# Reordered first loads, a first weight cast in four parts, a first v cast on two engines, and re-timed fillers

## The chip, the cores and the metric

The kernel runs on one core of a Trainium2 chip. The metric is device time in microseconds (us), the median of several executions. "The trace" is the record of one profiled execution, in which times count from the start of the span. The span (about 297 us here) is a little shorter than the timed execution. Engines are abbreviated as in the profile: PE is TensorE, PEld its weight loads, DVE VectorE, ACT ScalarE, POOL GpSimd, SP SyncE, which issues the transfers.

## The reference

The computation is a retention layer (attention with a decay in place of softmax) followed by a feed-forward layer with a squared ReLU. Cut to what matters:

```python
# q, k, v: [8 batches, 8 heads, 576, 64] float32; w_in [512, 2048]; w_out [2048, 512]
scores = q @ k.T / 8
ret    = (scores * Dmat) @ v                  # Dmat: gamma_h ** (i - j), lower triangle
x      = ret, heads side by side              # [4608, 512]
h      = x @ w_in
out    = maximum(h, 0)**2 @ w_out             # [4608, 512]
```

## The kernel before

The tokens are handled in 18 groups of 256. Each group's q, k, v are loaded, cast to float16, transposed, turned into scores, masked, and multiplied out to `xT`. Then 64 matmuls on `w_in` (called feed-forward matmuls below), the squared ReLU, and the output matmuls on `w_out` follow. In the first groups the output matmuls are 128x512. Later ones replace part of them by sums of matrices (a Strassen scheme), so that VectorE forms sums `gS` for TensorE.

The order of all instructions is fixed when the program is built. A list scheduler simulates the five engines with a **modelled duration** for each task and always starts the ready task of smallest key. A duration in the model is not a wait on the chip, but it decides the order in which instructions are put into each engine's queue.

```python
FIRST = ["p0", "p2", "w0", "w1", "w2", ..., "w7", "p4", "p6"]     # loads, in this order
...
for i in range(WARM):        # 40 filler matmuls, taken only when nothing else is ready
    fill.append(add("PE", 10 ** 6, 0.43 if i < 8 else 0.216, warm, ...))
...
# a pair of groups: k, q, v, one load each of 512 KB
loaded[name, u] = loaded[name, u + 1] = dma_task(0, 1.6 if loaded else 3.0, fn, ...)
...
# a weight block of 1 MB: cast in two halves, one by GpSimd, one by ScalarE
for j, eng in enumerate(("POOL", "ACT")): ...
...
# the casts of a pair: both halves of the first pair's v on VectorE
eng = "DVE" if (lead if name != "v" else (lead or e)) else "POOL"
```

Loads called w0 to w3 are the blocks of `w_in`, w4 to w7 those of `w_out`. The "third pair" is the one loaded after the weights.

## Time and profile before

| what | before |
|---|---|
| median of 3 runs | 299.49 us (299.16 to 299.77) |
| span of the profiled run | 296.8 us |
| TensorE busy | 285.9 us, 96% |
| VectorE, ScalarE, GpSimd busy | 196.5, 187.3, 92.1 us |
| DMA engines full | from 3 to about 46 us |

The busy shares say that TensorE is the resource, and that only some 11 us of the span are not covered by it. Where those lie is read in the slices and stretches that the prediction shows. In a timeline line, the columns are the start, the time that the piece took, engine, source line, operation, output and inputs, and the count. A bracket gives the engine's idle time before the piece, and what ended it.

### The profile page before, as it was taken

Reading aid. Unit: us, or ns where it says so; the run is one execution under the profiler, and the core shown is the slowest. Engines: PE = TensorE matmul, PEld = TensorE weight load, DVE = VectorE, ACT = ScalarE, POOL = GpSimd, SP = SyncE. Lnnn points to the kernel's source line nnn. Section 1 sums busy time; section 2 is a strip of 40 time slices with the busy share of each in tenths; the row PEclk is TensorE's granted clock in tenths of the full one; section 3 lists DMA queues with packets and bytes.
Section 4 is the critical chain, followed back from the end, with each engine's and each line's share of the span. In section 5 each row is a group of like instructions: output and inputs, shape, how many; then the busy total and the mean of one; then the engine's idle time right before and its main releaser. Section 6 shows DMA issues by size and latency. Waiting matters only on the chain.

```text
span 296.8 us, 10046 instructions
## 1 busy us (share of the span) xinstructions
PE 285.9 (96%) x4320; PEld 233.8 (79%) x4320; DVE 196.5 (66%) x414; ACT 187.3 (63%) x353; POOL 92.1 (31%) x127
## 2 busy tenths in 40 slices
PE   8969989999999999999999999999999999999995
PEld 3558745687878888888888888888888888888874
DVE  4597479859395939593949598766777876462410
ACT  4348753484857666657576666666676856658861
POOL 4433396434242424152514142233433410000000
PEclk9999999999999999999999999999999999999999
DMA  7999997999887989898979597989999960101012
GB/s 202 310 388 385 362 300 207 185 224 164 209 162 195 185 195 207 198 179 202 176 181 177 142 181 188 184 187 202 184 217 203 180 140 2 73 3 71 2 71 73
DMA packets 139261, 54.14 MB, mean 182 GB/s; under 512 B 118096, under 2 KB 130640, under 8 KB 139216
## 3 DMA queue, kind: packets, MB, share of 16 engines
q1 hardware_dynamic: 138768, 52.97, 81.6%
q8 instruction: 34, 0.56, 0.8%
q10 hardware_dynamic: 448, 0.52, 0.6%
q14 instruction: 11, 0.09, 0.1%
HBM read 36.70 MB, written 9.44 MB: 155 GB/s over the span
## 4 chain that ended last, share of the span: by engine, by line
PE 67%; DMA 12%; DVE 10%; ACT 6%; issue 2%; POOL 2%; SPq 0%; DVEq 0%; POOLq 0%
PE ph L807 29%; PE po L900 26%; DVE gS L878 6%; PE po L848 5%; PE psO L331 4%; DMA wo<-in_moe_w_out_dram 4%; ACT gT L825 3%; DMA pair<-in_k_dram 3%; ACT rl L815 3%; DMA wi<-in_moe_w_in_dram 3%; DMA pair<-in_v_dram 2%; DVE rT L629 1%; PE psc L331 1%; PE psS L331 1%; POOL qx L391 1%
## 5 line engine op out<-in xcount | busy, mean ns | idle before, releaser
L807 PE MATMUL ph<-xT,w_in 128*128 128x256 f16 x1152 | 139.0, 273 | 1.1 <-POOL w_in L313 1.1
L807 PEld LDWEIGHTS <-w_in 128*128 128x128 f16 x1152 | 111.2, 98 | 15.7 <-POOL w_in L313 1.4
L815 ACT ACTIVATE rl<-ph 128x512 f16<-128x512 f32 x144 | 83.9, 588 | 49.2 <-PE ph L807 45.7
L825 ACT ACTIVATE gT<-rl 128x512 f16<-128x512 f16 x112 | 70.5, 630 | 3.5
L878 DVE TENSOR_TENSOR gS<-gT 128x512 f16<-128x512 f16 x60 | 28.9, 485 | 42.6 <-ACT gT L825 42.0
L900 PEld LDWEIGHTS <-gS 128*128 128x128 f16 x480 | 45.7, 98 | 8.5 <-DVE gS L878 3.0
L900 PE MATMUL po<-wT,gS 128*128 128x256 f16 x360 | 49.2, 273 | 1.1 <-DVE gS L878 1.1
L355 POOL TENSOR_TENSOR v<-v,vdec_full 128x512 f16<-128x512 f32 x24 | 25.6, 1067 | 46.8 <-DMA v<-in_v_dram 43.0
L900 PEld LDWEIGHTS <-gT 128*128 128x128 f16 x360 | 34.9, 98 | 4.3
L343 POOL CAST kq<-k 128x512 f16<-128x512 f32 x28 | 19.1, 684 | 44.7 <-DMA k<-in_k_dram 39.0
L900 PE MATMUL po<-w_out,gT 128*128 128x256 f16 x240 | 31.1, 273 | 0.0
L343 POOL CAST kq<-q 128x512 f16<-128x512 f32 x28 | 18.7, 667 | 26.7 <-DMA q<-in_q_dram 26.6
L827 DVE TENSOR_TENSOR gT<-rl 128x512 f16<-128x512 f16 x32 | 16.2, 510 | 13.8 <-ACT rl L815 13.4
L848 PE MATMUL po<-w_out,gT 128*128 128x512 f16 (+1 forms) x112 | 22.9, 349 | 0.2 <-POOL w_out L313 0.2
L690 DVE TENSOR_TENSOR xT<-psO,gam_full 128x512 f16<-128x512 f32 x28 | 18.4, 684 | 4.6 <-PE psO L331 4.5
L913 ACT COPY u<-po 128x256 f32<-128x256 f32 x30 | 11.0, 366 | 13.4 <-PE po L900 13.3
L878 DVE TENSOR_TENSOR gS<-gS,gT 128x512 f16<-128x512 f16 x30 | 18.1, 604 | 1.0
L629 DVE TENSOR_TENSOR rT<-psc,mask 128x512 f16<-128x512 f32 x28 | 18.6, 680 | 0.3 <-PE psc L331 0.3
L923 DVE TENSOR_TENSOR o<-po,u 128x256 f32<-128x256 f32 x30 | 12.5, 418 | 9.3 <-PE po L900 5.3
L878 DVE TENSOR_TENSOR gS<-gT,gS 128x512 f16<-128x512 f16 x30 | 16.4, 548 | 1.0
L848 PEld LDWEIGHTS <-gT 128*128 128x128 f16 x112 | 10.6, 98 | 7.9 <-issue 0.4
L900 PE MATMUL po<-w_out,gS 128*128 128x256 f16 x120 | 15.8, 273 | 0.0
(78 smaller groups left out, 264.2 us busy)
## 6 DMA issues: line engine op xcount, KB each, us to landing
out_dram<-o SPq DMA_DIRECT2D x31, 256.0 KB, 2.7
k<-in_k_dram SPq DMA_DIRECT2D x24, 256.0 KB, 4.6
q<-in_q_dram SPq DMA_DIRECT2D x24, 256.0 KB, 4.4
v<-in_v_dram SPq DMA_DIRECT2D x24, 256.0 KB, 4.5
wi<-in_moe_w_in_dram SPq DMA_DIRECT2D x4, 1024.0 KB, 9.4
wo<-in_moe_w_out_dram SPq DMA_DIRECT2D x4, 1024.0 KB, 9.6
pair<-in_k_dram SPq DMA_DIRECT2D x4, 512.0 KB, 8.0
pair<-in_q_dram SPq DMA_DIRECT2D x4, 512.0 KB, 7.4
```

The costliest lines, as they stand in the source:

```text
L331: nc.tensor.matmul(out_, lhsT=lhsT, rhs=rhs, start=start, stop=True, skip_group_check=True, tile_position=(64 * row, 64 * col))
L343: op(out=out_.rearrange("p (n b a d) -> p n b a d", n=2, b=2, a=2), in_=in_.rearrange("p (n a b) d -> p n b a d", n=2, a=2))
L355: nc.gpsimd.tensor_tensor(out=t, in0=tile_of["v32", u], in1=vdec[kind].rearrange("p (h o) -> p h o", o=1).to_broadcast([P, H, D]), op=ALU. ...
L629: nc.vector.tensor_tensor(out=r, in0=tile_of["psc", g][:, :, cols(s)].rearrange("p a (n i) -> p a n i", i=64), in1=mask.rearrange("p (o r ...
L690: nc.vector.tensor_tensor(out=tile_of["x", g][:, :, s * P:(s + 1) * P].rearrange("p n (c i) -> p c n i", c=2), in0=tile_of["psO", g][:, :, ...
L807: nc.tensor.matmul(tile_of["ph", g, fb][:, j, :], lhsT=w_in16[:, m, fi * P:(fi + 1) * P], rhs=tile_of["x", g][:, m, :], start=(m == 0), st ...
L815: nc.scalar.activation(out=t, in_=tile_of["ph", g, fb], func=ACTF.Relu)
L825: nc.scalar.activation(out=t, in_=rl, func=ACTF.Square)
L827: nc.vector.tensor_tensor(out=t, in0=rl, in1=rl, op=ALU.mult)
L848: nc.tensor.matmul(tile_of["po", u, lo], lhsT=tile_of["g", g][:, fi, s * P:(s + 1) * P], rhs=w_out16[:, fi, lo:hi], start=(fi == 0), stop= ...
L878: nc.vector.tensor_tensor(out=Sx(k, h), in0=in0(h), in1=in1(h), op=op)
L900: nc.tensor.matmul(tile_of["pb", g, bank], lhsT=left(i), rhs=right[:, i, :], start=(start and i == 0), stop=(i == HF - 1), skip_group_chec ...
```

## The change

The intent is to start feed-forward work earlier. TensorE stood idle for 2.28 us between 16 and 22 us, so the first weight block is taken ahead of the second pair's v and cast in four quarters. The first pair's v is shared by two engines, the transposes no longer wait for v's cast, and fillers stand where their cold (slow) duration puts them. Beside that, one line alters the modelled duration of a load.

```diff
-    FIRST = ["p0", "p2", "w0", "w1", ..., "w7", "p4", "p6"]
+    FIRST = ["k0", "q0", "v0", "k2", "q2", "w0", "v2", "w1", ..., "w7", "k4", "q4", "v4", "k6", "q6", "v6"]
...
-        fill.append(add("PE", 10 ** 6, 0.43 if i < 8 else 0.216, warm, ...
+        fill.append(add("PE", 10 ** 6, 1.75 if i == 0 else 0.43 if i < 15 else 0.216, warm, ...
...
-            loaded[name, u] = loaded[name, u + 1] = dma_task(0, 1.6 if loaded else 3.0, fn, ...
+        loaded[name, u] = loaded[name, u + 1] = dma_task(0, 1.81 if loaded else 2.9, fn, ...
...
+        parts = 2 if i == 0 else 1                     # weight block 0 in four casts
+        for part in range(parts): ...
...
-                eng = "DVE" if (lead if name != "v" else (lead or e)) else "POOL"
+                eng = "DVE" if (e if name == "v" else lead) else "POOL"
...
-                xs[name].append(add(eng, base + i + e / 2, dur, fc, ...
+                xs[name].append(add(eng, base + (7 if name == "v" else i + e / 2), dur, fc, ...
...
+        return w[:2] if fi < 2 else w                  # the first matmuls need two quarters only
```

More of the change, by code (lines that the diff above doesn't have):

```diff
@@ L227 @@
     PAIRED = 8
-    FIRST = ["p0", "p2", "w0", "w1", "w2", "w3", "w4", "w5", "w6", "w7", "p4", "p6"]
+    FIRST = ["k0", "q0", "v0", "k2", "q2", "w0", "v2", "w1", "w2", "w3", "w4", "w5", "w6", "w7", "k4", "q4", "v4", "k6", "q6", "v6"]
     sched = Schedule(dict(ff=4, prS=1, prO=1, g=3, ld=5, wst=4, kq=7, v16=7, rT=4, x=3, rl=3, o=4, p1=1, u2=1, u4=1,
@@ L243 @@
     for i in range(WARM):
-        fill.append(add("PE", 10 ** 6, 0.43 if i < 8 else 0.216, warm, deps=fill[-1:], acq=() if fill else ("ff",)))
+        fill.append(add("PE", 10 ** 6, 1.75 if i == 0 else 0.43 if i < 15 else 0.216, warm, deps=fill[-1:], acq=() if fill else ("ff",)))
     sched.free("ff", fill[-1:])
@@ L282, in add_load, with add_load_pair, fn @@
             loaded[name, u] = dma_task(0, 1.2 if loaded else 2.1, fn, acq=("ld",) if n == 0 else ())
-    def add_load_pair(u):
+    def add_load_pair(name, u):
         b, c = units[u][1:]
-        for n, (name, src) in enumerate((("k", k), ("q", q), ("v", v))):
-            def fn(n=n, name=name, src=src):
-                if name != "q":
-                    tile_of["stage", u] = stage.tile([P, 2, H, 2 * D], FP32, name="pair", tag="wst")
-                x = tile_of[name + "32", u] = tile_of["stage", u][:, n % 2]
-                nc.sync.dma_start(out=x, in_=src[b, :, c * P:(c + 2) * P, :].rearrange("h (p e) d -> p h (e d)", e=2))
-            loaded[name, u] = loaded[name, u + 1] = dma_task(0, 1.6 if loaded else 3.0, fn,
-                                                             acq=("wst",) if name != "q" else ())
+        n = "kqv".index(name)
+        def fn():
+            if name != "q":
+                tile_of["stage", u] = stage.tile([P, 2, H, 2 * D], FP32, name="pair", tag="wst")
+            x = tile_of[name + "32", u] = tile_of["stage", u][:, n % 2]
+            nc.sync.dma_start(out=x, in_=(k, q, v)[n][b, :, c * P:(c + 2) * P, :].rearrange("h (p e) d -> p h (e d)", e=2))
+        loaded[name, u] = loaded[name, u + 1] = dma_task(0, 1.81 if loaded else 2.9, fn, acq=("wst",) if name != "q" else ())
     def add_weight(i):
@@ L309, in add_weight, with fc @@
         halves = []
-        for j, eng in enumerate(("POOL", "ACT")):
-            def fc(j=j, eng=eng):
-                s = tile_of["w", i]
-                (nc.gpsimd.tensor_copy if eng == "POOL" else nc.scalar.copy)(
-                    out=dst[:, 2 * j:2 * j + 2], in_=s[:, 2 * j:2 * j + 2])
-            halves.append(add(eng, -50 + i, 1.2 if eng == "POOL" else 1.0, fc, deps=[t]))
+        parts = 2 if i == 0 else 1
+        for part in range(parts):
+            sl = slice(part * 512 // parts, (part + 1) * 512 // parts)
+            for j, eng in enumerate(("POOL", "ACT")):
+                def fc(j=j, eng=eng, sl=sl):
+                    s = tile_of["w", i]
+                    (nc.gpsimd.tensor_copy if eng == "POOL" else nc.scalar.copy)(
+                        out=dst[:, 2 * j:2 * j + 2, sl], in_=s[:, 2 * j:2 * j + 2, sl])
+                halves.append(add(eng, -50 + i, (1.05 if eng == "POOL" else 1.0) / parts, fc, deps=[t]))
         sched.free("wst", halves)
@@ L319 @@
     for x in FIRST:
-        (add_load_pair if x[0] == "p" else add_weight)(int(x[1:]))
+        if x[0] == "w":
+            add_weight(int(x[1:]))
+        else:
+            add_load_pair(x[0], int(x[1:]))
     for u in range(NU):
@@ L378, in add_unit_pair @@
             for e in range(2):
-                eng = "DVE" if (lead if name != "v" else (lead or e)) else "POOL"
+                eng = "DVE" if (e if name == "v" else lead) else "POOL"
                 def fc(name=name, e=e, eng=eng):
-                    if e == 0:
+                    if (name + "x", u) not in tile_of:
                         tile_of[name + "x", u] = cast.tile([P, 2, H * D], FP16, name=name + "x", tag="kq16")
@@ L393, in add_unit_pair @@
                 dur = (dict(POOL=1.1, DVE=0.6) if name == "v" else dict(POOL=0.62, DVE=0.4))[eng]
-                xs[name].append(add(eng, base + i + e / 2, dur, fc, deps=[loaded[name, u]] + xs[name],
+                xs[name].append(add(eng, base + (7 if name == "v" else i + e / 2), dur, fc, deps=[loaded[name, u]],
                                     acq=() if e else ("kq",)))
+            if xs[name][0]["eng"] == xs[name][1]["eng"]:
+                sched.need(xs[name][1], xs[name][0])
         sched.free("wst", xs["k"] + xs["q"])
@@ L404, in ft @@
                         nc.tensor.transpose(t[:, e, x, :], tile_of[name + "x", u][:, e, x * P:(x + 1) * P], ident)
-            t = add("PE", base + 2 + i, 0.45, ft, deps=[xs[name][-1]], acq=("ff",))
+            t = add("PE", base + 2 + i, 0.45, ft, deps=xs[name], acq=("ff",))
             if name == "q":
@@ L421, in add_unit_pair @@
             sched.free("ff", es)
-        T["kvx", u] = [xs["k"][-1], xs["v"][-1]]
+        T["kvx", u] = xs["k"] + xs["v"]
     def add_ret_pair(g):
@@ L791, with wcast_of @@
     T["ff2"] = []
+    def wcast_of(fi):
+        w = wcast[fi // 4]
+        return w[:2] if fi < 2 else w
     def add_ff(g):
@@ L809, in add_ff @@
                 f1.append(add("PE", base + (nf * fb + j) * n, 0.01 + 0.2133 * n, f,
-                              deps=[T["x", u] for u in us] + wcast[(nf * fb + j) // 4] + f1[-1:],
+                              deps=[T["x", u] for u in us] + wcast_of(nf * fb + j) + f1[-1:],
                               acq=("ff",) if j == 0 else ()))
```

## The prediction

> **What bounds the kernel now.** I began with the busy slices of the page, to find the phases.
>
> ```profile
> PE   8969989999999999999999999999999999999995
> DMA  7999997999887989898979597989999960101012
> ```
>
> TensorE is at nine tenths almost everywhere; the soft slices are the third (14.8 to 22.3 us) and the sixth. The DMA engines are full through the sixth slice (44.5 us). So I asked for busy time per stretch over the first 50 us, and added the idle of TensorE after that: 0.37 us in 60 to 70, 0.8 in 80 to 100, 0.6 in 100 to 150, 0.5 in 150 to 200, next to none to 290. What a start-up change can win lies before 45 us.
>
> ```profile
> core 0: us, PE busy (x) PEld busy (x) DVE busy (x) ACT busy (x) POOL busy (x), PEclk, DMA share, GB/s
> 16.00:18.00 2.00, 1.35 (x86) 1.14 (x83) 2.00 (x5) 1.17 (x2) 1.04 (x1) 1.00 1.04 389
> 18.00:20.00 2.00, 1.51 (x28) 1.31 (x29) 1.53 (x4) 0.00 (x0) 0.00 (x0) 1.00 1.05 388
> 20.00:22.00 2.00, 0.86 (x9) 0.54 (x7) 1.97 (x6) 1.19 (x2) 1.04 (x1) 1.00 1.06 388
> ...
> 38.00:40.00 2.00, 1.79 (x10) 0.68 (x7) 1.39 (x3) 1.65 (x4) 1.31 (x2) 1.00 1.17 287
> 40.00:42.00 2.00, 1.38 (x13) 0.76 (x12) 2.00 (x3) 0.39 (x1) 2.00 (x3) 1.00 1.07 290
> ```
>
> TensorE idles 2.28 us in 16 to 22 us, the hole that the change aims at, and 0.83 us in 38 to 42. All the while the DMA share is over 1. Next, the chain that ended last, in order of time, to see which of the two decides:
>
> ```profile
> 8.49 8.18 DMA wi<-in_moe_w_in_dram
> ...
> 17.80 11.05 DMA wo<-in_moe_w_out_dram
> ...
> 29.98 8.84 DMA pair<-in_k_dram
> ...
> 38.97 1.69 POOL kx L391 x2
> ```
>
> From 2 to 39 us the chain is transfers handing buffers to transfers; then GpSimd's casts of the third pair. It reaches TensorE only at 43.2 us. TensorE's own order of time says how much slack it has against that chain:
>
> ```profile
> 36.65 1.47 PE L807 MATMUL ph<-xT,w_in 128*128 128x256 f16 x12
> 38.33 1.89 PE L848 MATMUL po<-w_out,gT 128*128 128x512 f16 x8 [0.21 <-POOL w_out L313]
> 40.17 0.40 PE L404 MATMUL psT<-ident,kx 128*128 128x128 f16 x4
> 41.18 0.40 PE L404 MATMUL psT<-ident,kx 128*128 128x128 f16 x4 [0.62 <-POOL kx L391]
> 41.41 1.24 PE L848 MATMUL po<-w_out,gT 128*128 128x512 f16 x5
> 42.49 0.39 PE L404 MATMUL psT<-ident,qx 128*128 128x128 f16 x4
> 43.21 0.40 PE L404 MATMUL psT<-ident,qx 128*128 128x128 f16 x4 [0.33 <-POOL qx L391]
> ```
>
> At 38.33 it waits 0.21 us for the last of the eight weight blocks, and then 0.62 and 0.33 us for GpSimd's casts. So it has caught up with the transfers at 38.3 us; whatever it does sooner before that, it waits longer there.
>
> **What the Trainium skill says.** "DMA: Bandwidth & Descriptors", section "Issuing engines are not separate DMA queues": all issues run on the same 16 DMA engines and interleave. The trace agrees: 291 GB/s while pair loads in 512 B pieces run, 388 GB/s for the weights in 2 KB pieces, with no gap from 3 to 46 us. A new order of loads then moves landings among themselves, not the last of them. The same page, "Why a DMA increments its semaphore by 16 and not by 1": the parts of a DMA finish independently, and all 16 are needed. The trace's landing records show it: of the second weight block 15 parts were in by 19.30 us and the last at 20.79. "Runtime: NRT & Kernel Launch", "Instruction fetch mechanics": instructions come in 16 KiB blocks by a DMA of the engine's own; here such a packet starts at 16.08 us, takes 1.12 us, and I take it for what held that one part back. "SBUF — State Buffer", "SBUF: two separate sides": a VectorE operation with two SBUF inputs and a GpSimd operation exclude each other. The decayed v cast takes VectorE 0.68 us at 15.96 with GpSimd idle and 1.09 us at 42.60 with GpSimd casting, which agrees in direction.
>
> **Part 1, the first weight block before v of the second pair.** Landings before: second k 10.4, second q 12.2, second v 14.0, w0 16.7, w1 20.8, w2 23.5, w3 26.1, then every 2.7 us to w7 at 37.0. The exchange brings w0 to 12.2 + 2.7 = 14.9 us and v to some 16.8; either is 1.35 us later if the delayed part falls to it. The bytes ahead of w1 are the same, so w1 stays at 20.8 and w7 at 37.0. The cast of w0, in halves of about 0.52 us (half of 1.04), is ready from 15.5 us instead of 17.8.
>
> **Part 2, v by two engines, transposes before v.** The first pair's v cost VectorE 1.29 us in series; now GpSimd takes 1.04 us beside VectorE's 0.68. With the copies of kT and qT first and fewer fillers ahead (11, 3 and 4 before the first scores, instead of 20, 6 and 7 plus one; 40 in all either way), the first transposes move from 7.9 to 6.0 us, where 11 cold fillers of 0.427 us end (1.26 + 4.7). The first scores move from 12.6 to about 9.2 us, behind a VectorE copy that in both pairs starts only after ScalarE's. The first group's output should start near 13.3 instead of 15.8 us, and its xT be ready by about 15.5 instead of 18.3. That also removes the 1.2 us pause in the second scores at 17.3 us, which I read as a wait for the PSUM tile that xT frees.
>
> **Part 3, what TensorE does with it.** The order of its instructions shows the catch. Before w1's cast at 21.9 us the old kernel has done the 16 feed-forward matmuls that need w0 only, and both pairs' scores and sums. The new one has done exactly the same, then runs five leftover fillers and stands at the first matmul that needs w1. The second group's output still comes behind w1 matmuls, after 12 of them instead of 8. So the useful work done at 21.9 us is equal: gain 0. From there to 38.3 us the order of large pieces is the same. What is gained is 0.2 us of wait before that output, since R is earlier, and this turns into a longer wait for w7.
>
> **Part 4, after w7.** The models' new durations shift the later order. Ten instead of 8 output matmuls run before the third pair's k transposes and 6 instead of 5 between k and q: three more of 0.2135 us in holes of 0.62 and 0.33 us, so TensorE is 0.64 us ahead at 43.4 us. I expect most of it back a little later. VectorE now copies qT before it casts v. In the old order the cast filled its time until the copy could start at 44.26; in the new order the copy (0.42), the cast (0.7 to 1.1) and a weight sum (0.7 to 1.1) come after 44.26, and the masks, which began at 46.38, begin at 46.1 to 46.7. The masks end 2.8 us later and the third group's output needs them. It began at 49.46; its new start lies between 49.2 and 49.8, with the same work done ahead of it (two output matmuls more, 0.43 us; eight transposes fewer, 0.45). So -0.3 to +0.3. Besides, the queue places the first store, ready at 40.0 us, ahead of the fourth pair's k, which had been issued at 36.85 and landed at 43.7: it will land near 45.3. GpSimd took it up at 44.55, and its transpose comes at 47.3, so that is hidden, narrowly.
>
> **Sum.** Start-up 0; wait at w7 absorbs up to 0.2; filled holes -0.64; VectorE's masks +0.3 to +0.6; later reordering of stores and sums 0, with 0.2 either way. Net -0.3 us on 299.49: 299.2.
>
> **Rivals.**
> - *The hole is recovered.* If the early w0 let TensorE do 2 us more by 22 us, and the weights kept ahead, the time would be 297.3. For it: the 2.28 us hole. Against it: the equal work counted above and the wait for w7, fed by a DMA queue that is never empty.
> - *The shift of the slow part.* If instruction packets fall on other DMA engines relative to the weights, w7 lands up to 1.35 us sooner or later, and the whole rest follows: 298.1 to 300.6. For it: 15 parts of w7 in by 36.84 and the first at 35.02, so stragglers set the landing. Against it: nearly the same instructions are consumed by that time.
> - *A new wait of v.* v lands two to four us later; if GpSimd, which now casts w0 first, makes the second sums late, TensorE, in order, reaches the w1 matmuls after 21.9 with its five fillers (1.07 us) in the way. My reckoning gives 21.6 at worst, so 0.3 us of slack; beyond it a loss of perhaps 0.5: 299.7.
> - *GpSimd or the late fourth k becomes the bound near 47 us:* plus 1 at most, 300.2.
>
> **Range and chances.** All rivals lie within 2.2 us, while 2% is 6.0 us; TensorE's whole idle time before 50 us is barely more than that, and most of it waits for the first landings, which do not move. So within 2% is nearly certain. The range takes the straggler rival to most of its extent: 298.1 to 300.3.
>
> **What would show it.** Right: w0's cast near 15.5, w1's still at 20.8 and the matmuls on it still near 21.9; w7's cast still at 37.1 and a wait before the output matmuls there of 0.2 us or more; smaller waits before the third pair's transposes; a wait for rx before the third group's output near 49.5. Wrong: w7 landing over half a microsecond off, or useful work before 21.9 that I did not count, or the third group's output beginning more than 0.4 us from 49.5.

## The result, and the profile after

| | before | after |
|---|---|---|
| median, 4 runs each | 299.53 us (299.16 to 299.77) | 298.90 us (297.94 to 299.04) |
| span of the profiled run | 296.8 us | 296.6 us |
| granted clock of the profiled run | 0.999 | 1.0 |

The ratio is 0.9973, 95% interval 0.9950 to 0.9996. All ratios are against the kernel before. The class is "same", as predicted.

First the busy slices of the changed kernel's page, in tenths, 7.4 us each.

```profile
PE   8979999999989999999999999999999999999995
DMA  7999998899999989999969698999898980101012
```

The sixth slice is now full, while the third is still soft. Next, busy time by stretch for the changed kernel (columns as in the prediction).

```profile
core 0: us, PE busy (x) PEld busy (x) DVE busy (x) ACT busy (x) POOL busy (x), PEclk, DMA share, GB/s
...
18.00:20.00 2.00, 0.47 (x37) 0.38 (x33) 1.82 (x3) 0.11 (x1) 1.46 (x1) 1.00 1.04 383
...
40.00:42.00 2.00, 1.69 (x15) 0.94 (x13) 2.00 (x3) 0.57 (x2) 2.00 (x3) 1.00 0.73 214
```

TensorE's start-up hole has not gone. It has been gathered into 18 to 20 us, where TensorE is idle for 1.53 us until the second pair's v, which now lands behind the first weight block, has been cast. Part of the rest of the old hole is covered by five fillers at 20.8 us, which count as busy but do no work. The hole at 40 to 42 us has halved, from 0.62 to 0.31 us of idle time. Here is the changed kernel's chain of work that ended last, in order of time (start, length, what):

```profile
8.50 9.41 DMA pair<-in_v_dram
...
19.55 9.14 DMA wo<-in_moe_w_out_dram
...
29.83 8.80 DMA pair<-in_k_dram
...
38.78 1.68 POOL kx L397 x2
```

It is the chain of before: transfers up to 38.6 us, then GpSimd's casts of the third pair. TensorE's timeline around it, changed kernel:

```profile
38.15 2.32 PE L860 MATMUL po<-w_out,gT 128*128 128x512 f16 x10
40.30 0.39 PE L412 MATMUL psT<-ident,kx 128*128 128x128 f16 x4
41.00 0.40 PE L412 MATMUL psT<-ident,kx 128*128 128x128 f16 x4 [0.31 <-POOL kx L397]
41.23 1.46 PE L860 MATMUL po<-w_out,gT 128*128 128x512 f16 x6
42.52 0.90 PE L412 MATMUL psT<-ident,qx 128*128 128x128 f16 x8
...
48.90 0.30 PE L337 MATMUL psO<-kqT,R 64*64 64x128 f16 x4 [0.19 <-DVE rx L455]
```

The listed waits of 0.21, 0.62 and 0.33 us of before have become one of 0.31: two output matmuls more stand ahead of the k transposes, and one more ahead of q's. This is the place where the two traces part. Up to it they agree. The second group's last feed-forward matmul starts at 37.85 us before and at 37.82 after.

The wait for the eighth weight block has not gone, though none is listed at 38.15 us. (The list counts from a modelled end of the matmul before, and leaves out gaps under 0.15 us.) GpSimd's cast of that block in the changed kernel:

```profile
36.88 1.21 POOL L316 CAST w_out<-wo 128x1024 f16<-128x1024 f32 x1 [1.70 <-DMA wo<-in_moe_w_out_dram]
```

It ends at 38.10 us, and the output matmul starts 0.05 us later, as it does before. From the start of the last feed-forward matmul to that of the output matmul are 0.33 us after and 0.49 before, where 0.11 is usual. So TensorE loses 0.22 us there after, and 0.38 before.

To follow it further I counted **TensorE's work done** by a given time in each trace: every matmul that has started (fillers left out) is counted with the spacing at which its kind runs back to back in the traces (0.216 us for 128x512, 0.109 for 128x256, 0.056 for a transpose, about 0.015 for a small matmul of the attention part). The whole kernel comes to 273.16 us in each of these traces. A difference in the table is time won or lost, to the grain of one large matmul. The labels are those of the experiments below.

| work done by | before | after | e2_late_old | e3_model_only | e11_old_durations |
|---|---|---|---|---|---|
| 28 us | 11.68 | 11.68 | 11.57 | 11.46 | 11.35 |
| 38 us | 21.58 | 21.58 | 21.58 | 21.47 | 21.14 |
| 44 us | 25.93 | 26.79 | 25.93 | 26.58 | 26.14 |
| 56 us | 37.12 | 37.88 | 37.23 | 37.77 | 36.91 |
| 64.5 us | 45.14 | 45.91 | 45.25 | 45.80 | 44.82 |
| 95 us | 74.13 | 75.55 | 74.67 | 75.44 | 75.22 |
| 150 us | 128.85 | 129.62 | 129.18 | 129.72 | 129.72 |
| 230 us | 209.56 | 209.78 | 208.15 | 210.22 | 209.46 |

So the changed kernel wins nothing by 38 us, 0.86 us from there to 44, still has 0.77 us of it at 56 and 64.5 us, 1.4 us at 95, and has given most of it back by 230 us.

### The profile page after: what moved, and what is told of

Same layout as the page of the kernel before. It is cut to its first block, busy times and chain, and to the rows that moved or that the text cites. A ratio compares the mean times of both kernels' runs of the same rounds, so it can differ in the third digit from the quotient of the medians.

```text
span 296.6 us, 10048 instructions
## 1 busy us (share of the span) xinstructions
PE 286.1 (96%) x4320; PEld 233.5 (79%) x4320; DVE 196.2 (66%) x413; ACT 187.5 (63%) x354; POOL 93.9 (32%) x129
## 4 chain that ended last, share of the span: by engine, by line
PE 64%; DVE 11%; ACT 10%; DMA 9%; issue 2%; POOL 2%; POOLq 0%
PE po L912 26%; PE ph L819 25%; DVE gS L890 5%; ACT rl L827 5%; ACT gT L837 4%; PE psO L337 4%; PE po L860 4%; DMA pair<-in_v_dram 3%; DMA wo<-in_moe_w_out_dram 3%; DMA pair<-in_k_dram 3%; PE warm L241 2%; DVE gT L839 2%; PE psc L337 1%; PE psS L337 1%; PE psT L412 1%
## 5 line engine op out<-in xcount | busy, mean ns | idle before, releaser
L890 DVE TENSOR_TENSOR gS<-gT 128x512 f16<-128x512 f16 x60 | 31.8, 531 | 40.3 <-ACT gT L837 39.7
L361 POOL TENSOR_TENSOR v<-v,vdec_full 128x512 f16<-128x512 f32 x24 | 26.2, 1092 | 58.4 <-DMA v<-in_v_dram 51.0
L839 DVE TENSOR_TENSOR gT<-rl 128x512 f16<-128x512 f16 x32 | 18.1, 568 | 13.8 <-ACT rl L827 13.4
L349 POOL CAST kq<-q 128x512 f16<-128x512 f32 x28 | 18.1, 647 | 23.3 <-DMA q<-in_q_dram 23.2
L925 ACT COPY u<-po 128x256 f32<-128x256 f32 x30 | 11.0, 367 | 15.5 <-PE po L912 15.4
L890 DVE TENSOR_TENSOR gS<-gS,gT 128x512 f16<-128x512 f16 x30 | 16.3, 544 | 1.0
L860 PEld LDWEIGHTS <-gT 128*128 128x128 f16 x112 | 10.6, 98 | 7.9 <-issue 0.2
L912 PE MATMUL po<-wT,gT 128*128 128x256 f16 x120 | 15.8, 273 | 0.0
L890 DVE TENSOR_TENSOR gS<-gT,gS 128x512 f16<-128x512 f16 x30 | 15.1, 505 | 1.0
```

Of the source, the lines that this page charges most:

```text
L349: op(out=out_.rearrange("p (n b a d) -> p n b a d", n=2, b=2, a=2), in_=in_.rearrange("p (n a b) d -> p n b a d", n=2, a=2))
L361: nc.gpsimd.tensor_tensor(out=t, in0=tile_of["v32", u], in1=vdec[kind].rearrange("p (h o) -> p h o", o=1).to_broadcast([P, H, D]), op=ALU. ...
L839: nc.vector.tensor_tensor(out=t, in0=rl, in1=rl, op=ALU.mult)
L860: nc.tensor.matmul(tile_of["po", u, lo], lhsT=tile_of["g", g][:, fi, s * P:(s + 1) * P], rhs=w_out16[:, fi, lo:hi], start=(fi == 0), stop= ...
L890: nc.vector.tensor_tensor(out=Sx(k, h), in0=in0(h), in1=in1(h), op=op)
L912: nc.tensor.matmul(tile_of["pb", g, bank], lhsT=left(i), rhs=right[:, i, :], start=(start and i == 0), stop=(i == HF - 1), skip_group_chec ...
```

## The experiments

My theory after the result had three parts. First, the start-up edits are worth nothing, since TensorE meets the transfers again at the eighth weight block. Second, the time won by 56 us comes from a different order of later instructions, which the line of load durations makes. Third, what comes after 56 us is a drift by chance, caused by GpSimd's casts falling on VectorE's sums. The rivals were that one of the start-up parts made the gain itself, and that the new order of the transfer queue did.

The results, with the kernel before run on the same chip in the same session each time (e1 to e4 on one chip, e5 to e12 on another). The last two columns give the start of the third group's first feed-forward matmul (before 56.02, after 55.24) and of the last group's last one (before 286.49, after 286.23).

| run | median us (range) | ratio, 95% interval | third group | end |
|---|---|---|---|---|
| e1_again | 298.63 (297.62 to 298.98) | 0.9996, 0.9969 to 1.0024 | 55.37 | 285.50 |
| e2_late_old | 299.03 (298.40 to 299.96) | 1.0011, 0.9984 to 1.0038 | 55.95 | 287.48 |
| e3_model_only | 298.52 (296.59 to 300.31) | 0.9984, 0.9947 to 1.0022 | 55.39 | 285.89 |
| e4_queue_old | 299.43 (297.95 to 300.62) | 1.0020, 0.9988 to 1.0052 | 55.75 | 287.77 |
| e5_w0_back | 298.25 (297.08 to 298.82) | 0.9976, 0.9947 to 1.0006 | 55.33 | 286.63 |
| e6_fillers_back | 298.37 (296.48 to 299.17) | 0.9976, 0.9937 to 1.0015 | 55.23 | 284.36 |
| e7_one_load_less | 295.62 (294.92 to 296.65) | 0.9896, 0.9869 to 0.9923 | 52.89 | 282.94 |
| e8_ten_fillers | 299.88 (299.22 to 301.63) | 1.0042, 0.9998 to 1.0086 | 57.05 | 288.28 |
| e9_gate2 | 364.09 (362.53 to 365.97) | 1.2188, 1.2138 to 1.2237 | 55.46 | 351.31 |
| e10_gate3 | 308.41 (307.55 to 312.12) | 1.0352, 1.0292 to 1.0411 | 55.15 | 294.95 |
| e11_old_durations | 298.16 (297.00 to 299.51) | 0.9977, 0.9934 to 1.0020 | (see there) | 286.18 |
| e12_first_v_old | 298.32 (298.19 to 299.10) | 0.9990, 0.9954 to 1.0025 | 55.40 | 286.95 |

The kernel before had medians of 298.69 us (297.57 to 300.22, 11 runs) beside e1 to e4, 298.83 (298.36 to 299.42, 7 runs) beside e5 to e8, and 298.81 (297.34 to 301.05, 11 runs) beside e9 to e12. Its own scatter is as large as the effect, which is why the verdicts below rest on milestones in the traces and not on the medians.

### e1_again: the changed order once more

The instruction order of the changed kernel is written down as a list for each engine, and the scheduler follows the list. Nothing else differs. This is the tool for the next runs, and the measure of the scatter.

```diff
+ORDER = {"PE": "warm#0 warm#1 ...", "POOL": "...", "SP": "...", "DVE": "...", "ACT": "..."}
...
-                    if all(self.count[r] >= ...
+                    if t["key"] == turn[e] and all(self.count[r] >= ...
```

> A control: the changed kernel, with each engine's order written out as a list instead of found by the scheduler; the instruction orders are the same to the last instruction. Both theories: the time of the changed kernel, 298.9 us, within 0.4; the third group's first feed-forward matmul at 55.2 us as before (old kernel: 56.0), within 0.2. What it differs by tells how far a trace and a time can be trusted.

The third group started at 55.37 us (0.13 later), the end came 0.73 us sooner than in the first trace of the same order, and on this chip the ratio was 0.9996 instead of 0.9973. So three quarters of a microsecond between two single traces, and a quarter of a per cent between two sessions, mean nothing by themselves (the two intervals overlap).

### e2_late_old: new start, old order later

In e1's lists, everything from the third pair's transposes and the fourth pair's loads on is put back into the order of before.

```diff
-    "PE": "... (new order) ..."
+    "PE": "... (new order up to the third pair's transposes, then the old one) ..."     # the same on all engines
```

> The new start-up with the old kernel's order on every engine from the third pair's transposes (and the fourth pair's loads) on. My theory, that the start-up is worth nothing and the late order everything: the third group's first feed-forward matmul at 55.8 to 56.0 us, hardly before the old kernel's 56.0, and a time within 0.3 us of the old kernel. Rival, that the earlier start is what gained: 55.2 us at that matmul and about 0.6 us off the total.

The third group's feed-forward started at 55.95 us, where before had it at 56.02. Work done by 56 us was 37.23 us, against 37.12. All of the start-up edits together, with the old order behind them, are worth 0.1 us. The median was 0.34 us above that of the kernel before, just outside the 0.3 expected.

### e3_model_only: one line of the change alone

```diff
-            ... = dma_task(0, 1.6 if loaded else 3.0, fn, ...
+            ... = dma_task(0, 1.81 if loaded else 2.9, fn, ...
```

> The old kernel with one line of the change only, the load durations in the scheduler's model (1.81 for 1.6, 2.9 for 3.0), which leaves the start-up's loads, casts and fillers practically as they were and gives the new order later. My theory: the third group's first feed-forward matmul at 55.2 to 55.5 us, and 0.4 to 0.8 us off the total, as with the whole change. Rival, that the start-up gained: 56.0 us and no gain.

The old kernel with these two numbers of the model started the third group at 55.39 us, with 37.77 us of work done by 56. Of the 0.4 to 0.8 us expected off the total, the medians show 0.17, so that part missed. The edit is less clean than the expectation says: the start changed too. Here also VectorE copies the first transposes before it casts v, and the first feed-forward matmul comes at 19.71 us (18.89 before, 16.44 after). By 38 us, however, the work done is that of before but for one matmul. Together with e2 this makes a square. By the start of the third group, the new order is worth about 0.6 us behind the old start and 0.7 behind the new one, and the new start 0.1 and 0.15.

A part of such differences comes from the transfers, which land a little sooner or later in each trace. The third pair's k landed at 38.82 us before, 38.63 after, 38.76 in e2 and 38.63 in e3. Counted from that landing, the third group starts after 17.20, 16.61, 17.19 and 16.76 us. So the new order is worth 0.44 us behind the old start and 0.58 behind the new one, and the new start 0.15 and 0.01 (with the new and with the old order behind it). In e1, e4, e5, e6 and e12, which keep the new order or nearly so, the same count gives 16.58 to 16.62 us. The granted clock of e3's profiled run was 0.994, lower than the others', so it is not what made it quick.

### e4_queue_old: old order in the transfer queue only

In e1's lists, only SyncE's (the issues of the loads and stores) is put back to the old order from the fourth pair's loads on.

```diff
-    "SP": "... add_weight.fn#7 (new order) ..."
+    "SP": "... add_weight.fn#7 (old order from the fourth pair's loads on) ..."
```

> The changed kernel with the DMA queue's old order from the fourth pair's loads on; all four compute engines keep the new order. My theory of the middle part: the fourth pair's k then lands near 43.5 instead of 44.5 us, GpSimd goes on casting without a pause, VectorE's decayed v cast takes 1.09 us again instead of 0.68, the masks start 0.3 us later and the third group's output at 49.2 to 49.4 instead of 48.9 us; some 0.3 us of the 0.78 gained at 55 us is lost there. Rival, that only TensorE's own order counts: 48.9 and 55.2 us as in the changed kernel.

This expectation missed. I had thought that VectorE's cast of the third pair's v took 0.68 us in the changed kernel, and 1.09 before, because GpSimd stood idle beside it, waiting for the fourth pair's late k (which landed at 44.49). With the old queue that k landed at 43.82 and GpSimd was casting from 44.43, yet VectorE's cast at 44.93 again took 0.68 us:

```profile
44.43 0.61 POOL L414 CAST kx<-pair 128x512 f16<-128x512 f32 x1
...
44.93 0.68 DVE L410 TENSOR_TENSOR vx<-pair,vdec_pair 128x512 f16<-128x512 f32 x1
...
44.98 1.10 POOL L414 CAST kx<-pair 128x512 f16<-128x512 f32 x1
```

What differs is which engine started first. VectorE's cast began as GpSimd's first cast was ending, 0.05 us ahead of the second, and it was that second cast which stretched, to 1.10 us. In the changed kernel VectorE's cast (44.42) was 0.20 us ahead of GpSimd's next one (44.62), which took 0.96. Before, VectorE's cast began at 42.60 inside a GpSimd cast (42.09 to 43.15), and ended 0.54 us after it. The third group's output, in e4, began 10.28 us after the third pair's k had landed, against 10.27 in the changed kernel and 10.64 before. So the queue order is not the cause. The kernel's 55.75 us, instead of 55.24, comes from w7, which landed at 37.34 instead of 36.83 us in this trace.

### e5_w0_back: the first weight block after v again

```diff
-    FIRST = [..., "k2", "q2", "w0", "v2", "w1", ...
+    FIRST = [..., "k2", "q2", "v2", "w0", "w1", ...
```

> The changed kernel with the first weight block back behind the second pair's v. My theory, that the place of w0 is worth nothing because w1 to w7 land as they did: w0's cast near 16.8 us, w1's cast still near 20.7, the third group's first feed-forward matmul at 55.3 us within 0.2, and the total of the changed kernel within the scatter. Rival, that the early w0 recovered TensorE's hole: 55.9 us and 0.5 us more in total.

The third group started at 55.33 us, against 55.24: w0's place is worth nothing. (w0 landed at 17.92 us and not near 16.8, since one of its 16 parts came 1.2 us after the others.) The trace shows the mechanism. TensorE was even 0.43 us ahead of the changed kernel at the second group's last feed-forward matmul (37.39 us), and lost it at the eighth weight block. From the timeline of TensorE in this run:

```profile
38.19 2.32 PE L860 MATMUL po<-w_out,gT 128*128 128x512 f16 x10 [0.53 <-POOL w_out L316]
```

It starts at 38.19 us, where the changed kernel had 38.15 and before 38.33. In all three traces this is 1.27 to 1.32 us after w7's landing.

### e6_fillers_back: old modelled length of the fillers

```diff
-        ... 1.75 if i == 0 else 0.43 if i < 15 else 0.216 ...
+        ... 0.43 if i < 8 else 0.216 ...
```

> The changed kernel with the old lengths of the fillers in the model, so 20 fillers stand ahead of the first transposes again and the start-up is late as in the old kernel. My theory: first scores back near 12 us, first feed-forward matmul a little later, but the third group's first feed-forward matmul still at 55.3 us within 0.2. Rival, that the earlier first group gained: 55.8 to 56.0 us.

The first transposes were back at 7.93 us (5.92 in the changed kernel), the first scores at 11.29 (8.75) and the first feed-forward matmul at 17.93 (16.44). Yet the third group started at 55.23, the same as the changed kernel. A start that is 1.5 to 2.5 us later cost nothing at that point: at the second group's last feed-forward matmul 0.48 us of it were left (38.30 us). The wait for w7, which is absent here, took up 0.22 of that, and the hole at the third pair's k transposes the rest. In e5, e6 and e12 the scheduler ran anew, so the order behind the start can differ a little from the changed kernel's. The end, 284.36 us, is even 1.9 us sooner than the changed kernel's. That is the drift discussed below.

### e7_one_load_less: do the transfers set it?

On e1's lists, the second pair's q is not loaded but taken from k. Its output is wrong, which doesn't matter for the time. (Relative error 0.42.) The number of instructions on the computing engines stays.

```diff
+            if (name, u) == ("q", 2):
+                tile_of["q32", u] = tile_of["k32", u]
+                return
```

> The changed kernel with all orders kept and one load left out: the second pair's q is taken from the k that is there already (a wrong result, on purpose), 512 KB or 1.8 us of transfer less ahead of all the weights. My theory, that the bytes in the queue set the time up to 39 us: w1's cast at 18.9, w7's at 35.1, the third group's first feed-forward matmul at 53.4 to 53.7 us, and 1.5 to 1.9 us off the total. Rival, that TensorE's work from the first weight on sets it and the transfer is hidden: 55.2 us, no gain.

This is the one run that moved far. Everything after it in the queue landed about 1.5 us sooner (w1 19.07 instead of 20.62 us, w7 35.29 instead of 36.83), and the third group started at 52.89, which is 2.35 us sooner. The gain was larger than expected (53.4 to 53.7, and 1.5 to 1.9 us off the total; the median fell by 3.2 us against the kernel before). TensorE was 1.11 us sooner at the second group's last feed-forward matmul. Then the waits vanished too: 0.22 us at w7, 0.48 and 0.29 at the third pair's k and q transposes, 0.25 at its masks, by the starts of the matmuls in both traces. In the chain of this run the transfers no longer occur:

```profile
1.25 4.88 PE warm L258 x11
...
35.67 1.31 PE ph L839 x12
36.98 2.16 PE po L880 x10
39.14 0.45 PE psT L432 x8
```

The 2.35 us stayed to the third and fourth groups (2.36 at 78 us), and the time fell by 1.0%. One load's worth of transfer before the weights is worth more than the whole change.

### e8_ten_fillers: how much slack does TensorE have against the transfers?

On e1's lists, ten more fillers stand before the first matmul that needs w1. At 0.213 us each they are 2.13 us.

```diff
-    "PE": "... warm#39 add_ff.f#4 ..."
+    "PE": "... warm#39 warm#40 warm#41 ... warm#49 add_ff.f#4 ..."
-    WARM = 40
+    WARM = 50
```

> The changed kernel with all orders kept and ten more fillers (10 times 0.2135, 2.1 us) in TensorE's stream just before the first matmul that needs the second weight block. My theory, that TensorE has only some 0.2 us to spare at the last weight block and some 0.4 us more in the waits behind it: the third group's first feed-forward matmul at 56.6 to 56.9 us and 1.3 to 1.7 us more in total. Rival, that the DMA queue alone decides and TensorE has room: 55.3 us and no loss.

The third group came at 57.05 us, 1.81 later, a little outside the expectation. (In total it was 1.05 us above the kernel before; the changed kernel was not run in that session.) By the third group's scores TensorE was only 1.17 us late: the waits at w7 and at the third pair's transposes had absorbed about 1 us. Then it lost most of that again in front of the fourth pair's k transposes (listed waits of 0.39 and 0.16 us at 48.75 and 49.31), because that k was issued at 42.21 instead of 40.27 us and landed at 47.96 instead of 44.49. Read with e5 this says that TensorE and the transfers are nearly in balance at 38 us. Being ahead by 0.4 us is lost in a wait, and being late by 2 us costs almost all of it. The idle 1.5 us at 18 to 20 us is therefore not spare time that a change may use up freely; it is only not worth removing alone.

### e9_gate2 and e10_gate3: an attempt at a kernel that beats both

After 56 us I had seen pairs of instructions that explain single waits. VectorE's sum `gS` takes 0.42 us when it is left alone. Three engines' timelines, before, 66 to 69 us:

```profile
66.51 1.24 POOL L355 TENSOR_TENSOR v<-v,vdec_full 128x512 f16<-128x512 f32 x1 [0.27 <-DMA v<-in_v_dram]
...
66.89 1.15 DVE L878 TENSOR_TENSOR gS<-gT 128x512 f16<-128x512 f16 x1
...
68.84 0.61 PE L900 MATMUL po<-wT,gS 128*128 128x256 f16 x4 [0.37 <-DVE gS L878]
```

The same engines in the changed kernel, 81 to 84 us:

```profile
81.10 1.04 POOL L361 TENSOR_TENSOR v<-v,vdec_full 128x512 f16<-128x512 f32 x1 [0.63 <-DMA v<-in_v_dram]
...
81.11 1.30 DVE L890 TENSOR_TENSOR gS<-gT 128x512 f16<-128x512 f16 x1
...
83.31 0.61 PE L912 MATMUL po<-wT,gS 128*128 128x256 f16 x4 [0.77 <-DVE gS L890]
```

In both, a sum that runs into GpSimd's decayed cast of v ends 0.28 us after that cast ends (67.75 to 68.03, and 82.14 to 82.42), and TensorE waits for the sums. The Trainium skill, "SBUF — State Buffer", section "SBUF: two separate sides", calls the port that the two engines share an exclusive lock, which whoever comes first holds for its whole instruction; these two pairs agree with it. Before's collision at 66.9 us is absent in the changed kernel, which gains 0.55 us more between 56 and 79 us; that the one makes the other is not shown. In e6_fillers_back the cast came at 81.78 us, after two of the three sums had begun, and TensorE did not wait:

```profile
81.78 1.07 POOL L361 TENSOR_TENSOR v<-v,vdec_full 128x512 f16<-128x512 f32 x1 [0.56 <-DMA v<-in_v_dram]
...
82.36 0.60 PE L912 MATMUL po<-wT,gS 128*128 128x256 f16 x4
```

So I tried to keep the casts off the sums by one dependence: the first k cast of a later group waits for the last sum of the group two (e9) or three (e10) before it.

```diff
+        T["s4", g] = s4[1]
...
+    for g in range(len(groups)):
+        if g >= 4 and ("s4", g - 2) in T:              # e10: g >= 5 and g - 3
+            sched.need(T["casts", units_of(g)[0]][0], T["s4", g - 2])
```

> The changed kernel with one dependence more: GpSimd's first k cast of a later group waits for the last Strassen sum of the group two before it, so that these casts fall less often on VectorE's sums of that group. Theory (after 56 us the time is moved by which of VectorE's sums of 0.42 us meet a GpSimd cast and stretch to 0.7 to 1.3 us, with TensorE waiting behind them): the summed excess of these sums over 0.42 us falls from the 11.6 to 14.9 us of the kernels so far to under 9, the stretch from the third group's first feed-forward matmul to the last group's last one falls from 230 to 231 us to about 229, and the time is 0.5 to 1.5 us under the changed kernel's, ratio 0.992 to 0.996. Rival (most of the stretched sums are hidden behind TensorE's other work, and casts that come later make the transposes and loads late): the excess may fall, but the stretch stays at 230 to 232 us and the ratio is 0.997 to 1.003. The start up to 56 us is that of the changed kernel in both.

> As the run with the gate two groups back, but the cast waits for the sum three groups back, which binds less. Theory: a part of the same gain, the excess of the sums over 0.42 us between 8 and 12 us, the stretch 229 to 230.5 us, ratio 0.994 to 0.998. Rival: as the changed kernel, 230 to 232 us, ratio 0.997 to 1.003.

Both missed badly, and further than even the rival had allowed: plus 22% and plus 3.5%. The sums hardly changed. Their total time above 0.42 us each (120 of them) was 13.3 us before, 12.9 after, 11.2 in e9 and 11.1 in e10, and e1_again and e11 had 11.6 without any gate. What the gate did was to close a circle: cast, transposes, scores, `xT`, feed-forward, sums, next cast. From the groups of the page of e9 (line, engine, operation; busy us and mean ns; idle us before, and its releaser):

```profile
L819 PE MATMUL ph<-xT,w_in 128*128 128x256 f16 x1152 | 148.9, 289 | 22.7 <-DVE xT L698 22.7
```

TensorE stands idle for 22.7 us in front of feed-forward matmuls because `xT` is late; in the changed kernel this idle time is 0.0. From the twelfth to the seventeenth group, each group of e9 costs 7 to 10 us more than before, and the granted clock in this profile was 0.947, so the circle need not be all of it. The circle is read from the dependences and this wait; no further run tests it. Neither kernel is a candidate, and no correct kernel of this study beats the changed one beyond its scatter. How much the collisions cost in all stays open. Two examples show what one of them can cost; the gate that was to remove them removed few.

### e11_old_durations: the change without the line of load durations

```diff
-        ... = dma_task(0, 1.81 if loaded else 2.9, fn, ...
+        ... = dma_task(0, 1.6 if loaded else 3.0, fn, ...
```

> The changed kernel with the old load durations (1.6 and 3.0) in the scheduler's model, nothing else. It is the converse of the run that put only the new durations into the old kernel. Theory (the half microsecond by 55 us comes from the later order that the new durations make): the third group's output starts 10.6 us after the fourth pair's neighbour k lands, as before the change (new order: 10.27), and the third group's first feed-forward matmul comes at 55.7 to 56.1 us. Rival (the parts of the start make it themselves): 10.2 to 10.3 us and 55.1 to 55.4 us. In both the whole time is within 0.4% of before's, because the later drift of 1 us covers it.

(The k meant there is the third pair's.) By the letter the expectation failed. The third group's output started 10.24 us after that k landed, not 10.6. The feed-forward milestone is not usable, since the scheduler found a third order here: the second group's last four feed-forward matmuls come only at 45.51 us, and the third group's first eight already at 51.56, ahead of output matmuls that the other orders take first. The count of work done is the measure that does not depend on this. It was 36.91 us by 56 us and 44.82 by 64.5, which is 0.2 and 0.3 us *less* than before. So the start-up edits alone, with the old durations, gain nothing here, which is what the theory says; by 95 us this order was 1.1 us ahead of before (75.22), which neither theory foresaw. The load durations are sufficient for the gain at 56 us (e3), but another order can come by a similar gain later.

### e12_first_v_old: the first v cast by VectorE alone

```diff
-                eng = "DVE" if (e if name == "v" else lead) else "POOL"
+                eng = "DVE" if (lead if name != "v" else (lead or e)) else "POOL"
```

> The changed kernel with both halves of the first pair's v cast on VectorE again, the rest unchanged. Theory (nothing gained before the last first-phase weights land is kept, since TensorE waits at the eighth weight block): the first output comes 0.3 to 1.0 us later than 13.40, the second group's last feed-forward matmul still lies at 37.8 to 38.0 and the third group's first one at 55.1 to 55.5 us. Rival (the two engines' cast is what gave the half microsecond): 55.7 to 56.1 us. Whole time within 0.4% of the changed kernel's in both.

The third group started at 55.40 us, within the theory's range and 0.16 from the changed kernel. The second group's last feed-forward matmul is 0.18 us later (38.00), and w7 landed 0.15 us later (36.98). The first output came at 13.53 us instead of 13.40, less than the 0.3 us at least that was expected. Sharing that cast is worth nothing at 56 us. The traces say why. In the changed kernel VectorE's half, which takes 0.68 us alone, takes 1.33 and ends 0.55 us after GpSimd's:

```profile
8.70 1.04 POOL L393 TENSOR_TENSOR vx<-pair,vdec_pair 128x512 f16<-128x512 f32 x1 [3.87 <-ACT kqT L423]
...
8.96 1.33 DVE L393 TENSOR_TENSOR vx<-pair,vdec_pair 128x512 f16<-128x512 f32 x1
```

and in e12 VectorE does both halves alone:

```profile
9.14 1.28 DVE L393 TENSOR_TENSOR vx<-pair,vdec_pair 128x512 f16<-128x512 f32 x2
```

Shared, the two casts take 1.59 us from first start to last end (8.70 to 10.29). VectorE alone takes 1.28.

## Why the prediction was right, and where a term was off

The time (299.2 predicted, 298.90 measured, range 298.1 to 300.3) and the class were right. That the time came within 0.3 us is in part luck: e1's two traces of one order end 0.73 us apart, and the predicted sum takes the favourable end of one of its terms (-0.64 and +0.3; the middle of that term would give about -0.2 us instead of -0.3). By its steps:

- **The bound up to 38 us: right.** Transfers, not TensorE, set the start. e7 shows it directly: one load less moved the third group by 2.35 us.
- **Parts 1 to 3, gain 0: right, and shown.** The work done at 28 and at 38 us is the same in both kernels, to the last digit of the table. w0's first quarters were ready at 15.55 us (the cast began at 14.94 and took 0.61; 15.5 predicted); the first output started at 13.40 (13.3 predicted); w1 landed at 20.62 (20.8) and its first matmul ran at 21.92 (21.9). e5, e6 and e12 undo three of the parts one by one, and the third group does not move by more than 0.16 us.
- **Part 2, the two engines beside each other: wrong, without effect.** It reckoned with GpSimd's 1.04 us *beside* VectorE's 0.68. VectorE's half took 1.33 us and ended 0.55 us after GpSimd's (see e12), although the prediction itself names a rule by which two such operations exclude each other.
- **The straggler: right in kind.** The part of a load that comes about 1.4 us late fell to one load more. Before, w1, w2 and w3 were each complete only 1.43 to 1.49 us after their first 15 parts; after, the second v, w1 and w2 (1.39 us each). Of that v 15 parts of 16 were in by 16.52 us and the last at 17.91. This is most of why TensorE idles 1.53 us at 18 to 20 us; GpSimd's half of the cast also took 1.46 us instead of 1.04, behind VectorE's. w7 shifted by 0.18 us only, so the rival of a shifted w7 did not happen.
- **A wait at w7 of 0.2 us or more: there, but not longer.** TensorE loses 0.22 us there (0.38 before), by the starts of its matmuls; it was no sooner at that place, and w7 landed 0.18 us sooner. e5 shows the longer wait (0.53 us listed) when TensorE is 0.43 us ahead.
- **Part 4, filled holes -0.64: right, a little small.** The listed waits fell from 0.21 + 0.62 + 0.33 to 0.31, which is -0.85, and the count of work done says -0.86 at 44 us. Some 0.2 us of it is the earlier landing of w7 and k, and not the new order.
- **Part 4, the term that was mis-sized: "VectorE's masks +0.3 to +0.6".** The prediction called wrong a third group's output more than 0.4 us from 49.5, and it began at 48.90. Counted from the landing of the third pair's k it began 0.37 us sooner than before (10.27 instead of 10.64), still just outside the predicted -0.3 to +0.3. The masks began at 46.04 us, just below the predicted 46.1 to 46.7. The two VectorE timelines show why. Before:

```profile
42.60 1.09 DVE L387 TENSOR_TENSOR vx<-pair,vdec_pair 128x512 f16<-128x512 f32 x1
...
46.38 1.29 DVE L447 TENSOR_TENSOR rx<-psc,mask 128x512 f16<-128x512 f32 x2 [0.69 <-PE psc L331]
```

and after:

```profile
44.42 0.68 DVE L393 TENSOR_TENSOR vx<-pair,vdec_pair 128x512 f16<-128x512 f32 x1
...
46.04 1.28 DVE L455 TENSOR_TENSOR rx<-psc,mask 128x512 f16<-128x512 f32 x2
```

The cast of v took 0.68 us and not up to 1.1, because it began ahead of GpSimd's next cast and not inside one (see e4). Before, the masks had waited 0.69 us for TensorE's scores, which now come 1.26 us sooner (44.65 instead of 45.91), 0.43 us of it because two output matmuls fewer stand ahead of them. When the third group's output starts, the same work is done in both traces (31.24 us), 0.56 us sooner after. So of the 0.86 us 0.3 was given back there, the low end of the term. What the sum had not foreseen is the way from there to the third group's first feed-forward matmul, where the lead is 0.78 us again: over the same work the kernel before takes 0.22 us longer. So by 56 us the term comes to about +0.1 instead of +0.3 to +0.6.
- **"Later reordering 0, with 0.2 either way": too narrow.** Between the third group's first and the fourth group's last feed-forward matmul the changed kernel gained another 0.55 us, and by the fifteenth group it had lost 1.1 of its 1.33 us again. e1 shows that one and the same order scatters as much: against the first trace, e1's was 0.45 us late at the end of the fifth group and 1.04 us early at the end of the twelfth. What a single trace shows after 56 us is thus not a property of the change.
- **Late fourth k:** predicted to land near 45.3 us and to be hidden; it landed at 44.49 and was hidden.

In sum, what the change was meant for is worth 0 to 0.2 us at 56 us. Some 0.4 to 0.6 us beside it was the work of the order that two numbers in a model bring about, and about 0.2 us that of transfers that happened to land sooner. Of the final 0.6 us of the medians no part can be told from the scatter between sessions.

## What to carry to other kernels

Before filling a hole at the start, look for the next place where the engine meets the transfers again: if it waits there, what it does sooner ahead of that place comes back as a wait. Taking one load away (e7), even with a wrong result, tells in one run what the transfers are worth. Where a scheduler orders the instructions, test every number of its model as a change of its own, and compare by work done at a milestone, since a later drift of a microsecond can hide or feign half a microsecond.

## What the Trainium skill lacked or had wrong

- "Runtime: NRT & Kernel Launch", "Instruction fetch mechanics", calls the cost of crossing a block of instructions mostly hidden. Here a load that a kernel waits for was 1.4 us later in the stretch where such a packet ran. Of the second v 15 parts of 16 were in by 16.52 us and the last at 17.91 (packet at 14.28 us); before the change the same happened to w1, 19.30 and 20.79 us (packet at 16.08). In each of the 14 traces one part trails the other 15 by 1.1 to 1.8 us for two to four loads in a row, beginning soon after the first such packet of the run (14.3 to 16.1 us) and ending with the loads around the second (21.0 to 24.3 us). That the packet is the cause is inferred from these times; no run took it away.
- "DMA: Bandwidth & Descriptors", "Specifications", gives 512 B and more as enough for line rate. In the trace of the kernel before, the loads in 512 B pieces moved at 291 GB/s (36 to 40 us, where nearly all packets are theirs) and the weights in 2 KB pieces at 388 (20 to 22 us).
- No page that I read says how much the time of one instruction order scatters from trace to trace: 0.73 us at the last feed-forward matmul here, and ratios of 0.9973 and 0.9996 in two sessions.
